# Expert slots of one fixed size, replaced by slots of falling sizes that the experts fill in the order of their token counts

## The chip, the cores and the metric

The kernel runs on one core of one Trainium2 chip. The metric is the device time of a run in microseconds: 519.92 us for the kernel before, the median of 3 runs (519.81 to 520.16). The profiled execution has a span of 518.1 us from its first instruction to its last.

## What is computed

A linear recurrence over 768 steps (4 batches, 8 heads, 48 values a head) makes 3072 rows of 384 values. A two-level gate then sends each row to one of 16 experts, and each expert is two matrix products with a ReLU between them. Cut to what matters:

```python
# recurrence, for each of 768 steps t
y[:, :, t] = r_t @ (state + (u * k_t) outer v_t)
state      = w * state + k_t outer v_t
# bridge: y becomes x, 3072 rows of 384
g_idx = argmax(x @ w_group);  g_w = softmax(x @ w_group)[g_idx]
for g in range(4):
    e_idx = argmax(xg @ w_expert[g]);  e_w = softmax(...)[e_idx]
    for e in range(4):                       # 16 experts in all
        h  = max(xg[mask_e] @ w1[g, e], 0)   # 384 -> 1024
        ye = h @ w2[g, e]                    # 1024 -> 384
        out[tok_idx] = g_w * e_w * ye
```

All numbers are 32-bit floats. How many rows an expert gets depends on the data. With the inputs that the reference sets up, the counts, from the largest to the smallest, are 211, 208, 207, 206, 200, 200, 199, 198, 195, 193, 185, 185, 183, 170, 170 and 162; they add up to 3072.

## The kernel before

The first stage computes the recurrence in 24 tiles of 128 rows, finds the expert of each row, and writes each finished row, by an indirect DMA, to the next free place in the region of its expert in DRAM (`x_sorted`). It keeps running counts in `cum`. A row carries its 384 values, its number and its gate.

```python
CAP = 224
region[e] = RG * e                          # first place of each expert in x_sorted
...
def rows(i):                                # a tile's rows to their places
    nc.gpsimd.indirect_dma_start(out=xs_dram, out_offset=place_i[:, i], in_=xt[:, i, :], ...)
...
for s in range(NT + LAST):                  # NT = 24 tiles; a tile runs through several steps s
    ...
    if s == 18:
        early[0] = load_expert(0, wpool)    # w1 and w2 of expert 0, on the SyncE queue
```

After the loop one number is made: whether an expert has more than 224 rows (or a decay lies outside the supported range). If so, a slow path at the end treats what is left.

```python
pc = ones.T @ cum[:, NT, :]                 # counts on all partitions
left = max(pc - region) >= CAP + 1 ...      # 8 small instructions on VectorE
```

The second stage takes the experts in the order 0 to 15. Each has a slot of 224 columns, in two parts of 128 and 96 rows, whatever its count; places that no token took hold zeros.

```python
NS = [P, CAP - P]                           # 128, 96
def load_rows(e):                           # xg: 3 buffers
    for j, n in enumerate(NS):
        nc.scalar.dma_start(out=xg[0:n, j, :], in_=xs_dram[RG*e + P*j : RG*e + P*j + n, :])
def columns(e):                             # transposes, rows to columns: px on TensorE, xe by VectorE
    ...transpose(px[:, i, P*j : P*j+n], xg[0:n, j, P*ko : P*(ko+1)], ident[0:n, 0:n])
    nc.vector.tensor_copy(xe[:, ...], px)
    # and on VectorE, from xg: ids (row numbers) and gates
def up(e, f):                               # two of 8 blocks of h; 3 matmuls each
    ...matmul(ph[:, i, :], lhsT=w1[:, ko, 128 columns], rhs=xe[:, ko, :])
    nc.scalar.activation(hT[:, f:f+2, :], ph, Relu)
def down(e, d):                             # one of 3 blocks of the output; 8 matmuls
    ...matmul(po, lhsT=w2[:, fo, 128 columns], rhs=hT[:, fo, :])
    nc.scalar.copy(yT[:, d, :], po)
def rows_out(e):                            # transposes back, gate, indirect DMA into out
    ...

load_rows(0); load_rows(1)
weights[1] = load_expert(1, pool)
columns(0)
for e in range(16):
    up(e, 0); up(e, 2)
    if e > 0: rows_out(e - 1)
    up(e, 4); up(e, 6)
    load_rows(e + 2)                        # cut: only where there is such an expert
    down(e, 0); columns(e + 1); down(e, 1); down(e, 2)
    weights[e + 2] = load_expert(e + 2, ...)
rows_out(15)
```

The order of TensorE's instructions is as written here; the other engines' instructions in the second stage are placed by the scheduler. Two sets of weights are held at a time. An expert is 24 matmuls in `up` and 24 in `down`, all with 128-column weights and 224 moving columns; in the trace each of them has two records, so 96 records an expert.

Of the kernel before, what the change touches and what calls it, by code (L numbers as in the profile page):

```python
# [8 lines left out]
FP32 = mybir.dt.float32  # L9
I32 = mybir.dt.int32  # L10
U32 = mybir.dt.uint32
AF = mybir.ActivationFunctionType
# [2 lines left out]

P = 128

CAP = 224

ROW_ID, ROW_GATE, ROW_EXTRA = 0, 1, 2  # L20

# [7 lines left out]
def kernel(  # L29
# [26 lines left out]
    FO = F // P  # L56
    NL = G + GE
    assert N == B * S and DM == H * D and B % 2 == 0 and H % 2 == 0 and S % P == 0 and D <= DP
    assert DM % P == 0 and F % P == 0 and G == Eg == 4 and DM <= 512 and NT * GE <= 512

    NX = N // P + GE
# [193 lines left out]
    def late_constants():  # L255
        nc.vector.tensor_scalar(out=start0, in0=region, scalar1=ident[:, 0:1], scalar2=None, op0=OP.mult)
        nc.vector.tensor_scalar(
            out=desc, in0=iota_f[:, 0:Eg], scalar1=-1.0, scalar2=float(Eg), op0=OP.mult, op1=OP.add
        )
        nc.vector.tensor_copy(cum[:, 0, :], start0)  # L260
        nc.vector.memset(nothing, 0.0)

        wlim = cst([1, H * D], "wlim")
        nc.vector.tensor_scalar(out=wlim, in0=wrow, scalar1=W_LEAST, scalar2=W_MOST, op0=OP.max, op1=OP.min)
        nc.vector.tensor_tensor(out=wlim, in0=wlim, in1=wrow, op=OP.is_equal)
        two = cst([1, 2], "two")
        nc.vector.reduce_sum(out=two[:, 0:1], in_=wlim, axis=AX)
        nc.vector.tensor_scalar(out=two[:, 1:2], in0=two[:, 0:1], scalar1=float(H * D), scalar2=None, op0=OP.is_ge)
        nc.vector.tensor_copy(ok_i, two[:, 1:2])

    def zero_places(j):

# [262 lines left out]
    own(0)  # L535
    todo = {}
    early = {}
    LAST = 5
    for s in range(NT + LAST):
        if s == NT + LAST - 2:  # L540

            for t in [t for t in sorted(todo) if t > s]:
                todo[s].extend(todo.pop(t))
        pieces = todo.pop(s, [])

        def run(when):
            for at, part in pieces:
                if at == when:
                    part()

        if s % 2 == 0 and s // 2 + 2 < NP:
            load_pair(s // 2 + 2)
        if s in (3, 5, 7, 9):
            zero_places(s // 2 - 1)
        if s == 18:
            early[0] = load_expert(0, wpool)
        run("first")
        if s < NT:
            turn(s)
            if s == 0:  # L560
                flipped(1)
                flipped(2)
            if s % 2 == 1 and s // 2 + 1 < NP:
                scale_k(s // 2 + 1, nc.gpsimd)
                own(s // 2 + 1)
        if 0 <= s - 1 < NT:
            own_values(s - 1)
        run("choice")
        if 0 <= s - 4 < NT:
            rows_T(s - 4)  # L570
        n = s - 5
        if 0 <= n < NT:
            row_logits(n)
        if 0 <= s - 3 < NT:
            back(s - 3)
        if 0 <= s - 2 < NT:
            values(s - 2)
        if s % 2 == 0 and s // 2 < NP:
            own_sum(s // 2)
        if s == 2:  # L580
            span_decay()
        run("last")
        if 0 <= s - 1 < NT:
            scores(s - 1)
        if s == 0:
            for t in R:
                nc.gpsimd.memset(t, 0.0)
        if s == 2:
            late_constants()
        if n in ROUTED:  # L590
            choice, before, gate, place, rows = routing(n)
            T = ROUTED[n]
            if n >= NT - B:
                choice()
                todo.setdefault(s + 1, []).extend(
                    [("last", part) for part in (before, gate, place)]
                    + [("last", lambda i=i, rows=rows: rows(i)) for i in range(T)]
                )
            else:
                todo.setdefault(s + 1, []).append(("choice", choice))  # L600
                todo.setdefault(s + 2, []).extend([("first", before), ("last", gate), ("last", place)])
                for i in range(T):
                    todo.setdefault(s + 3 + i, []).append(("last", lambda i=i, rows=rows: rows(i)))
    for _, part in todo.pop(NT + LAST):
        part()
    written.close()
    alive.close()


    left_i = cst([1, 1], "left_i", I32)  # L610
    pc = bank([P, GE], "pc")
    nc.tensor.matmul(pc, lhsT=ones, rhs=cum[:, NT, :], start=True, stop=True)
    cnt = cst([1, GE], "cnt")
    nc.vector.tensor_sub(cnt, pc[0:1, :], region[0:1, :])
    left = cst([1, 2], "left")
    nc.vector.reduce_max(out=left[:, 0:1], in_=cnt, axis=AX)
    nc.vector.tensor_copy(left[:, 1:2], ok_i)
    nc.vector.tensor_scalar(
        out=left[:, 1:2], in0=left[:, 1:2], scalar1=-float(2 * N), scalar2=float(2 * N), op0=OP.mult, op1=OP.add
    )  # L620
    nc.vector.tensor_add(left[:, 0:1], left[:, 0:1], left[:, 1:2])
    nc.vector.tensor_scalar(out=left[:, 0:1], in0=left[:, 0:1], scalar1=float(CAP + 1), scalar2=None, op0=OP.is_ge)
    nc.vector.tensor_copy(left_i, left[:, 0:1])


    NS = [P, CAP - P]
    with tc.tile_pool(name="moe", bufs=2, reuse_waits="tile") as pool:
        weights, xgs, xes, keys, hTs, yTs = {}, {}, {}, {}, {}, {}

        def load_rows(e):  # L630
            xg = xgs[e] = pool.tile([P, 2, XW], FP32, tag="xg", bufs=3, name="xg")
            for j, n in enumerate(NS):
                nc.scalar.dma_start(out=xg[0:n, j, :], in_=xs_dram[RG * e + P * j : RG * e + P * j + n, :])

        def columns(e):
            xg = xgs[e]
            xe = xes[e] = pool.tile([P, KO, CAP], FP32, tag="xe", name="xe")
            for ks in (range(0, 2), range(2, KO)):
                px = bank([P, len(ks), CAP], "px")
                for i, ko in enumerate(ks):  # L640
                    for j, n in enumerate(NS):
                        nc.tensor.transpose(  # L642
                            px[:, i, P * j : P * j + n], xg[0:n, j, P * ko : P * (ko + 1)], ident[0:n, 0:n]
                        )
                nc.vector.tensor_copy(xe[:, ks[0] : ks[-1] + 1, :], px)  # L645
            ids = pool.tile([P, 2], U32, tag="ids", bufs=4, name="ids")
            gates = pool.tile([P, 2], FP32, tag="gates", bufs=4, name="gates")
            for j, n in enumerate(NS):
                nc.vector.tensor_scalar(
                    out=ids[0:n, j : j + 1], in0=xg[0:n, j, DM + ROW_ID : DM + ROW_ID + 1], scalar1=float(N),  # L650
                    scalar2=None, op0=OP.add,
# [4 lines left out]
        def up(e, f):  # L656
# [1 line left out]
            if f == 0:  # L658
                hTs[e] = pool.tile([P, FO, CAP], FP32, tag="hT", name="hT")
            w1, xe = weights[e][0], xes[e]  # L660
            ph = bank([P, 2, CAP], "ph")
            for i in range(2):
                for ko in range(KO):
                    nc.tensor.matmul(  # L664
                        ph[:, i, :], lhsT=w1[:, ko, P * (f + i) : P * (f + i + 1)], rhs=xe[:, ko, :],
                        start=(ko == 0), stop=(ko == KO - 1), skip_group_check=True,
                    )
            nc.scalar.activation(hTs[e][:, f : f + 2, :], ph, AF.Relu)  # L668

        def down(e, d):  # L670

            if d == 0:
                yTs[e] = pool.tile([P, KO, CAP], FP32, tag="yT", name="yT")
            w2, hT = weights[e][1], hTs[e]
            po = bank([P, CAP], "po")
            for fo in range(FO):
                nc.tensor.matmul(  # L677
                    po, lhsT=w2[:, fo, P * d : P * (d + 1)], rhs=hT[:, fo, :], start=(fo == 0), stop=(fo == FO - 1)
                )
            nc.scalar.copy(yTs[e][:, d, :], po)  # L680

        def rows_out(e):
            yT, (ids, gates) = yTs.pop(e), keys.pop(e)
            for j, n in enumerate(NS):
                pb = bank([P, DM], "pb")
                for d in range(KO):
                    nc.tensor.transpose(pb[0:n, P * d : P * (d + 1)], yT[:, d, P * j : P * j + n], ident)  # L687
# [11 lines left out]
            tc.add_to_no_dep_group("rows out", ins.ins)  # L699

        with tc.manual_schedule(engines={mybir.EngineType.PE}):
            for e in range(2):
                load_rows(e)
            weights[0] = early.pop(0)
            weights[1] = load_expert(1, pool)
            columns(0)
            for e in range(GE):
                up(e, 0)
# [3 lines left out]
                up(e, 4)  # L712
                up(e, 6)
                if e + 2 < GE:
                    load_rows(e + 2)
                down(e, 0)
                if e + 1 < GE:
                    columns(e + 1)
                down(e, 1)
                down(e, 2)  # L720
                if e + 2 < GE:
                    weights[e + 2] = load_expert(e + 2, pool if e % 2 else wpool)
            rows_out(GE - 1)

    more = nc.values_load(left_i[0:1, 0:1], min_val=0, max_val=1, skip_runtime_bounds_check_because="a comparison")
    with tc.If(more > 0, preferred_fallthrough_block=False):  # L726
        with tc.tile_pool(name="rest", bufs=1) as rest:
            room = rest.tile([P, 1], FP32, name="room")
            nc.vector.memset(room, float(CAP))
            ok = nc.values_load(  # L730
                ok_i[0:1, 0:1], min_val=0, max_val=1, skip_runtime_bounds_check_because="a comparison"
            )
# [80 lines left out]
            ends = tl([P, GE], "ends")  # L813
            nc.vector.tensor_copy(ends, pc)
            begins = tl([P, GE], "begins")
            nc.vector.tensor_scalar(out=begins, in0=region, scalar1=room[:, 0:1], scalar2=None, op0=OP.add)
            nx = tl([P, GE], "nx")
            nc.vector.tensor_sub(nx, ends, begins)
            nc.vector.tensor_scalar(out=nx, in0=nx, scalar1=0.0, scalar2=float(P - 1), op0=OP.max, op1=OP.add)
# [117 lines left out]
```

## Time and profile before

| what | value |
|---|---|
| time, median of 3 runs | 519.92 us |
| span of the profiled execution | 518.1 us |
| TensorE busy, matmuls | 472.7 us, 91% |
| VectorE, ScalarE, GpSimdE busy | 32%, 27%, 24% |
| moved by DMA | 85.88 MB, 166 GB/s over the span |
| mean granted TensorE clock | 0.961 of full speed |
| first stage: last scatter to `x_sorted` starts at | 186.79 us |
| second stage: first transpose, first `up` matmul start at | 192.44, 195.12 us |
| last indirect DMA to the output starts at | 510.81 us |

A row of the costliest groups reads: line, engine, operation, tiles written and read, shape and number of instructions, then busy time in us and the mean of one in ns, then the engine's idle time just before them and what ended it. The busy times of overlapping records of a group are not counted twice, so a group's busy time may be far below number times mean: matmuls follow each other before the earlier one has drained. The timeline merges neighbouring records of a kind; its first two columns are the start and the duration in us.

### The profile page before, as it was taken

What the parts mean: (1) busy time and instruction counts of PE and PEld (TensorE: products, weight loads), DVE (VectorE), ACT (ScalarE), POOL (GpSimd) and SP (SyncE); (2) the same over time, 40 slices, a digit from 0 to 9 for tenths busy, and PEclk for the clock granted to TensorE, in tenths of its full rate; (3) what the DMA queues carried; (4) which work ended last, traced back from release to release, by engine and by line L of the source; (5) the groups of instructions that cost most, each with busy time, mean ns of one, the idle gap of its engine ahead of it and who ended that gap; (6) DMA issues with size and microseconds to landing.
All of it is one profiled execution on the core that took longest, in us unless ns stands there. A gap on an engine that the chain in (4) does not pass through costs nothing. (4 is left out here: it accounts for less than half of the span.)

```text
span 518.1 us, 8753 instructions
## 1 busy us (share of the span) xinstructions
PE 472.7 (91%) x3533; PEld 454.6 (88%) x3533; DVE 165.1 (32%) x493; ACT 138.1 (27%) x400; POOL 124.7 (24%) x113
## 2 busy tenths in 40 slices
PE   1679999999999629999999999999999999999992
PEld 1568988899999518999999999999999999999992
DVE  4377577877685721011011011011011011010000
ACT  1446545555554201111111111111111111111110
POOL 1874445555543230011011011011011011011011
PEclk9889999999999657999999999999999999999997
DMA  9978989557005441564674574574574564464000
GB/s 193 221 165 206 200 194 198 142 120 279 32 34 184 152 158 42 190 244 153 191 245 156 191 246 152 191 244 150 190 246 150 190 245 151 163 225 147 1 27 26
DMA packets 110613, 85.88 MB, mean 166 GB/s; under 512 B 78475, under 2 KB 102161, under 8 KB 110566
## 3 DMA queue, kind: packets, MB, share of 16 engines
q1 hardware_dynamic: 93228, 63.71, 41.9%
q10 hardware_dynamic: 14010, 12.09, 8.8%
q0 software_dynamic: 3328, 9.47, 5.1%
q8 instruction: 29, 0.48, 0.4%
q14 instruction: 18, 0.15, 0.1%
HBM read 70.25 MB, written 15.78 MB: 166 GB/s over the span
## 5 line engine op out<-in xcount | busy, mean ns | idle before, releaser
L664 PE MATMUL ph<-xe,w 128*128 128x224 f32 x768 | 153.2, 357 | 1.1 <-DVE xe L645 1.1
L677 PE MATMUL po<-hT,w 128*128 128x224 f32 x768 | 150.7, 353 | 0.0
L664 PEld LDWEIGHTS ph<-xe,w 128*128 128x128 f32 x768 | 146.3, 193 | 1.9 <-DVE xe L645 1.4
L677 PEld LDWEIGHTS po<-hT,w 128*128 128x128 f32 x768 | 144.2, 190 | 0.0
L694 POOL DMA_INDIRECT out_dram<-yt,ids x32 | 30.6, 956 | 293.4 <-DVE yt L689 288.5
L668 ACT ACTIVATE hT<-ph 128x448 f32<-128x448 f32 x64 | 34.8, 544 | 138.3 <-PE ph L664 138.3
L689 DVE TENSOR_SCALAR yt<-pb,gates 128x384 f32<-128x384 f32 (+1 forms) x32 | 18.2, 611 | 167.0 <-PE pb L687 167.0
L680 ACT COPY yT<-po 128x224 f32<-128x224 f32 x48 | 16.6, 346 | 134.7 <-PE po L677 99.0
L416 ACT ACTIVATE dv<-vt,du 128x48 f32<-128x48 f32 x192 | 45.9, 324 | 2.2 <-DVE du L410 2.2
L645 DVE COPY xe<-px 128x448 f32<-128x448 f32 (+1 forms) x32 | 14.7, 502 | 66.5 <-PE px L642 66.5
L405 POOL TENSOR_TENSOR dg<-rt,kt 128x768 f32<-128x768 f32 x12 | 22.0, 1831 | 49.3 <-DVE du L410 49.0
L446 DVE TENSOR_TENSOR am<-pa,later 128x512 f32<-128x512 f32 x48 | 30.9, 685 | 7.0 <-PE pa L441 6.7
L441 PE MATMUL pa<-rT,kT 48*128 48x128 f32 x384 | 29.3, 288 | 2.3 <-DVE rT L429 1.5
L360 POOL DMA_INDIRECT x_sorted<-xt,place_i x24 | 23.8, 992 | 28.1 <-DVE rb L316 13.6
L463 PE MATMUL py<-am,vt 128*64 128x128 f32 x384 | 28.3, 285 | 1.8 <-DVE am L446 1.7
L441 PEld LDWEIGHTS pa<-rT,kT 48*128 48x128 f32 x384 | 24.4, 190 | 4.5 <-DVE rT L429 1.7
L463 PEld LDWEIGHTS py<-am,vt 128*64 128x64 f32 x384 | 21.9, 140 | 5.6 <-DVE am L446 2.5
L431 ACT COPY kT<-pk 128x512 f32<-128x512 f32 x24 | 14.1, 588 | 46.2 <-PE pk L427 37.6
L400 POOL TENSOR_TENSOR kh<-kt,T 128x768 f32<-128x768 f32 (+1 forms) x12 | 21.7, 1806 | 12.9 <-ACT T L204 10.9
L406 POOL TENSOR_TENSOR dg<-dg,ub 128x768 f32<-128x768 f32 x12 | 21.8, 1819 | 0.9
L457 PE MATMUL py<-rT,R 128*128 128x128 f32 x160 | 21.3, 276 | 0.4 <-DVE at L354 0.4
L389 PEld LDWEIGHTS rb<-gw,xT 128*128 128x128 f32 x144 | 19.2, 203 | 2.9 <-issue 2.9
(112 smaller groups left out, 389.2 us busy)
## 6 DMA issues: line engine op xcount, KB each, us to landing
w<-in_moe_w_dram SPq DMA_DIRECT2D x32, 1536.0 KB, 6.4
x_sorted<-nothing ACTq DMA_DIRECT2D x4, 1351.0 KB
rt<-in_r_dram SPq DMA_DIRECT2D x12, 384.0 KB, 6.4
vt<-in_v_dram SPq DMA_DIRECT2D x12, 384.0 KB, 7.7
kt<-in_k_dram SPq DMA_DIRECT2D x10, 384.0 KB, 5.7
xg<-x_sorted ACTq DMA_DIRECT2D x16, 193.0 KB, 2.6
xg<-x_sorted ACTq DMA_DIRECT2D x16, 144.8 KB, 3.4
kt<-in_k_dram ACTq DMA_DIRECT2D x2, 384.0 KB, 5.5
```

What stands on the lines that cost most here:

```text
L360: ins = nc.gpsimd.indirect_dma_start(out=xs_dram, out_offset=bass.IndirectOffsetOnAxis(ap=place_i[:, i : i + 1], axis=0), in_=xt[:, i, :], ...
L400: engine.tensor_mul(khs[g % (RING - 1)][:, a0:a1, :, 0:D], kts[g % RING][:, a0:a1], spread(T2[m], 1, a1 - a0))
L405: nc.gpsimd.tensor_mul(dg, rts[g % RING][:, :, :, 0:D], kts[g % RING])
L406: nc.gpsimd.tensor_mul(dg, dg, spread(ub, 1, 2))
L416: nc.scalar.mul(dv[:, h, :], vts[g % (RING + 1)][:, a, h, 0:D], dvs[g][:, a, h : h + 1])
L441: nc.tensor.matmul(pa[e][:, hc, :], lhsT=kT[rows, hc, :], rhs=rT[rows, hc, :], start=True, stop=True, skip_group_check=True,)
L446: nc.vector.tensor_mul(am[:, e], pa[e], spread(later, 1, HP))
L463: nc.tensor.matmul(py[DP * e : DP * (e + 1), hc, :], lhsT=vt[:, a, 2 * hc + e, :], rhs=am[:, e, hc, :], start=(c == 0), stop=True, skip_gr ...
L664: nc.tensor.matmul(ph[:, i, :], lhsT=w1[:, ko, P * (f + i) : P * (f + i + 1)], rhs=xe[:, ko, :], start=(ko == 0), stop=(ko == KO - 1), ski ...
L668: nc.scalar.activation(hTs[e][:, f : f + 2, :], ph, AF.Relu)
L677: nc.tensor.matmul(po, lhsT=w2[:, fo, P * d : P * (d + 1)], rhs=hT[:, fo, :], start=(fo == 0), stop=(fo == FO - 1))
L694: ins = nc.gpsimd.indirect_dma_start(out=out, out_offset=bass.IndirectOffsetOnAxis(ap=ids, axis=0), in_=yt, in_offset=None, bounds_check=N ...
```

## The change

The sixteen slots get fixed, falling sizes. On the chip, the experts are sorted by their counts, and the largest expert takes the largest slot, and so on. Which expert a slot holds is then known only at run time, so the addresses of its rows in `x_sorted` and of its weights come from registers that are loaded from the sorted list. The slots are sized so that fewer columns are computed, while the largest of them has more room than before. The weights of the first slot have to start loading before all counts are known, so its expert is picked from the counts of the first 16 tiles and kept first.

```diff
-CAP = 224
+SLOTS = [256, 240, 229, 220, 214, 212, 206, 202, 199, 196, 193, 190, 187, 184, 178, 173]
+CAP = max(SLOTS)
+FOUR = 4
...
+    def key_constants():                        # once, in step 2
+        nc.vector.scalar_tensor_tensor(out=key_base, in0=region, scalar=-float(GE), in1=iota_f[:, 0:GE], ...)
+        nc.vector.tensor_scalar(out=key_base, in0=key_base, scalar1=float(GE - 1), ...)
+        for i, n in enumerate(SLOTS):
+            nc.gpsimd.memset(most[:, i : i + 1], ...)
+    def token_keys(i):                          # count * 16 + (15 - expert), on all partitions
+        nc.tensor.matmul(pc[:, 0, :], lhsT=ones, rhs=cum[:, i, :], start=True, stop=True)
+        nc.vector.scalar_tensor_tensor(out=pc[:, 1, :], in0=pc[:, 0, :], scalar=float(GE), in1=key_base, ...)
+    def pick_first():
+        keys = token_keys(FOUR * B)
+        nc.vector.reduce_max(out=top, in_=keys, axis=AX)
+        nc.vector.tensor_scalar(out=is_first, in0=keys, scalar1=top, scalar2=FIRST, ...)
+        nc.vector.tensor_copy(first_i, top)
+        number_of(first_i, first_i)             # one more VectorE instruction
...
-        if s == 18:
-            early[0] = load_expert(0, wpool)
+        if s == FOUR * B + 6:                   # 22
+            pieces.append(("last", pick_first))
+        if s == FOUR * B + 7:                   # 23
+            early[0] = load_expert(expert_of(first_i[0:1, 0:1], (SP,)), wpool)
...
+    keys = token_keys(NT)                       # after the last tile
+    nc.vector.tensor_add(keys, keys, is_first)
+    nc.vector.max(out=sorted_key[:, 0:8], in_=keys)
+    nc.vector.match_replace(out=keys, in_to_replace=sorted_key[:, 0:8], in_values=keys, imm_value=-1.0)
+    nc.vector.max(out=sorted_key[:, 8:16], in_=keys)
+    nc.vector.tensor_copy(order_i, sorted_key)
+    number_of(order_i, order_i)
+    ... # then the comparison with the room of each slot, in place of that with CAP
-    NS = [P, CAP - P]
+        def parts(e):
+            return [P, SLOTS[e] - P]
-        def load_rows(e):
+        def load_rows(e, engine, queue):
+            expert = expert_of(number(e), (engine,))        # register load
...
-                nc.scalar.dma_start(out=xg[0:n, j, :], in_=xs_dram[RG * e + P * j : RG * e + P * j + n, :])
+                queue.dma_start(out=xg[0:n, j, :], in_=by_expert[bass.ds(expert, 1), P * j : P * j + n, :]...)
... # transposes, up, down and rows_out: CAP -> SLOTS[e], NS -> parts(e)
-            for e in range(2):
-                load_rows(e)
+            load_rows(0, ACT, nc.scalar)
+            load_rows(1, ACT, nc.scalar)
-            weights[1] = load_expert(1, pool)
+            weights[1] = load_expert(expert_of(number(1), (SP,)), pool)
...
-                    load_rows(e + 2)
+                    expert = load_rows(e + 2, SP, nc.sync)
...
-                    weights[e + 2] = load_expert(e + 2, pool if e % 2 else wpool)
+                    weights[e + 2] = load_expert(expert, pool if e % 2 else wpool)
```

The slow path at the end is changed to know the room of each slot.

## The prediction

> **What bounds the kernel now.** I read the page's busy line first, then busy time by stretch, then the timeline of one expert.
>
> ```profile
> PE 472.7 (91%) x3533; PEld 454.6 (88%) x3533; DVE 165.1 (32%) x493; ACT 138.1 (27%) x400; POOL 124.7 (24%) x113
> L664 PE MATMUL ph<-xe,w 128*128 128x224 f32 x768 | 153.2, 357 | 1.1 <-DVE xe L645 1.1
> L677 PE MATMUL po<-hT,w 128*128 128x224 f32 x768 | 150.7, 353 | 0.0
> ```
>
> The two groups are the experts' products: 153.2 + 150.7 = 303.9 us of a 518.1 us span, with 1.1 us of idle time ahead of them. The busy time by stretch (stretch, its length, busy us of PE, PEld, DVE, ACT and POOL, granted clock, DMA share, GB/s) shows the same:
>
> ```profile
> 190.00:208.00 18.00, 14.47 (x59) 13.38 (x60) 2.44 (x18) 2.18 (x4) 0.00 (x0) 0.70 0.27 78
> 230.00:250.00 20.00, 20.00 (x114) 19.90 (x113) 2.94 (x9) 3.33 (x8) 1.92 (x2) 1.00 0.59 201
> 450.00:500.00 50.00, 50.00 (x279) 49.76 (x278) 5.25 (x10) 8.95 (x19) 5.74 (x6) 1.00 0.34 114
> ```
>
> From about 207 us to the end TensorE is never idle, at full clock, while the DMA engines are at 0.59 and the others below a fifth. So in this stage the time is TensorE's, and the question is what sets the pace of its matmuls: the moving columns, which the change cuts, or the weight loads, which it keeps. A busy PEld alone does not tell, since loads wait for the matmuls ahead of them. The timeline does:
>
> ```profile
> 493.38 0.82 PE L687 MATMUL pb<-ident,yT 128*128 128x128 f32 x6
> 498.57 9.24 PE L677 MATMUL po<-hT,w 128*128 128x224 f32 x48
> ```
>
> Of 48 records in 9.24 us the last ends 0.353 us after it starts (mean of the group), so starts are (9.24 - 0.353) / 47 = 0.189 us apart with 224 columns. With 128 columns it is (0.82 - 0.274) / 5 = 0.109 us. The slope is (0.189 - 0.109) / 96 = 0.83 ns a column. Half of the 128-column records also load 128 columns of weights, so a weight load fits in 0.109 us: down to 128 columns it is not the limit. The smallest slot has 173.
>
> **What the Trainium skill says.** "TensorE: Matmul & The Clock Gate", section "Back-to-back issue gap", gives N/2.4 + 2.5 ns warm for one pass. A record here takes 189 ns for 224 columns, which is 2 x 224/2.4 + 2.5 = 189.2: the trace agrees if a 32-bit record is two passes. The same section also gives sustained figures of about 81 ns at 128 columns and 131 at 512, a slope of only 0.13 ns a column; the 109 and 189 ns of this trace do not follow it, and the trace decides. The section "LDWEIGHTS (loading the stationary operand)" gives columns/1.2, an estimate of 107 ns for 128 columns, just what the 109 ns above allow. "DMA: Bandwidth & Descriptors", section "Why a DMA increments its semaphore by 16 and not by 1", says that a transfer is split over the largest number of engines, up to 16, that divides its slowest dimension. With parts of 128 and 96 rows nothing in the trace before could show this; it matters for a rival below.
>
> **The change, part by part.**
>
> *Removed: columns.* The slots add up to 3279 columns, before they were 16 x 224 = 3584: 305 fewer. Each costs 0.83 ns in each of an expert's 96 records: 305 x 96 x 0.83 ns = 24.3 us, all on TensorE, so all on the path. An expert now takes 96 x 0.189 + about 1.3 us of transposes = 19.4 us, which is the distance of equal points in the timeline. The last slot, with 173 columns, should take 96 x (0.189 - 51 x 0.00083) + 1.3 = 15.4 us, the first, with 256, 22.0 us. The transposes stay: back-transposes move 128 columns whatever the slot, and those into columns are six short ones an expert.
>
> *The slots hold.* All counts of these inputs lie at or below their slots, with the expert that leads after 16 tiles put first (206 rows in 256; then 211 in 240, 208 in 229, 207 in 220 and so on, 162 in 173; the tightest have 3 to 5 places free). So the slow path at the end stays off, as before.
>
> *Added in the first stage.* Two VectorE instructions and 16 tiny GpSimdE memsets in step 2, and five VectorE instructions of about 0.17 us with one matmul in step 22. GpSimdE idles up to 6.7 us a few steps later, and at step 22 TensorE has other tiles' work. I take 0.3 us for all.
>
> *Added between the stages.* The sort is seven VectorE instructions up to the order, some 0.2 us each going by their neighbours (0.15 to 0.18 us): from the last place at 186.0 us to about 187.5. A register load takes about 0.5 us here (0.47 to 0.54 us at the end of the program). The rows cannot be read before the last scatter has landed anyway, at 189.8. So the sort itself is hidden. What it moves is not:
>
> ```profile
> 189.81 5.10 ACTq L633 DMA_DIRECT2D xg<-x_sorted  x8
> 192.44 1.59 PE L642 MATMUL px<-ident,xg 128*128 128x128 f32 x6 [7.99 <-DMA xg<-x_sorted]
> 194.32 0.15 DVE L649 TENSOR_SCALAR ids<-xg 128x1 uint32<-128x1 f32 x1 [1.26 <-DMA xg<-x_sorted]
> 194.45 0.91 DVE L645 COPY xe<-px 128x448 f32<-128x448 f32 x2
> 195.12 12.10 PE L664 MATMUL ph<-xe,w 128*128 128x224 f32 x48 [1.09 <-DVE xe L645]
> ```
>
> TensorE starts the experts only after VectorE's copy at 194.45, and that copy stood behind an instruction that waited for the rows of the *second* expert, landed at 194.3. The instruction order of the changed kernel has the same order on VectorE. Before, the second expert's weights were under way by 156 and 169 us, and the row loads had the DMA engines to themselves. Now these 3.1 MB can start only once the order is known, around 189 us, and run beside the row loads. In the middle of the stage, where rows do run beside weights, they take a median of 3.4 and up to 4.7 us to land, against 2.6 for the first at 189.8. With the register load ahead of the second expert's rows (0.5 us), I put the start of the experts 2 us later, at about 197. The cold clock of this stretch (0.70) costs the same as before.
>
> *Moved: the first slot's weights*, from step 18 (about 120 us) to step 23, where they can start once the pick is made, near 157 us. A half of an expert's weights lands in 6.4 us, so they are there by about 172, over 20 us early.
>
> Sum: 519.9 - 24.3 + 0.3 + 2.0 = 497.9, say 498 us.
>
> **The rivals.**
>
> *The weights become the bound.* An expert's weights are 2 x 1536 KB. SyncE's queue waits for TensorE and not the other way round:
>
> ```profile
> SPq L373 <- PE ph L664: 135.1, 14, 14.4
> SPq L374 <- PE po L677: 129.4, 14, 9.3
> ```
>
> Two halves of 6.4 us[...] need under 13 us, and the shortest slot with a load behind it takes over 16 us. At 0.59 of the DMA engines for 19.4 us the same bytes need about 0.7 at 16.3 us. Against the rival; if it were so, the late slots would stop near 17.5 us and the time would be about 502.
>
> *Row loads on one DMA engine.* Second parts of 101, 71 and 59 rows divide by no number up to 16, so by the skill's rule they would go through one engine. At 201 GB/s and 0.59 busy, an engine moves 201/0.59/16 = 21 GB/s; 101 rows of 1544 bytes are then 7.4 us, 71 are 5.2. They also sit behind half a set of weights (4.7 us) in the same queue, and VectorE has the numbers of slot e+2 ahead of the copy for slot e+1. They would land some 13 us after the start of slot e, which lasts 17 to 18 us there: just hidden. At half that speed each of three slots would stall 1 to 2 us: about 501.
>
> *The weight load sets the pace after all.* Then 173 to 224 columns would gain nothing and 256 would cost: about 521. The 0.109 us records speak against it.
>
> *A longer wait at the start.* If the rows wait behind the whole 3.1 MB (about 9 us), the start moves by up to 5 us: about 501.
>
> **Range and chances.** The 24.3 us are an extrapolation within a measured slope and should hold to half a microsecond; the start could be anywhere from 0.5 to 4 us late, and the rows on one engine may add 3. That gives 495.5 to 501. Faster by over 2% means below 509.5; only a mechanism I have overlooked would miss that: 0.95, within 2% 0.03, slower 0.02.
>
> **What would show it.** Starts of matmuls 0.216 us apart at 256 columns and 0.147 at 173; the two product groups together at about 280 us busy; no idle time ahead of them beyond the first; the first expert matmul near 197 us, with VectorE waiting for the second slot's rows before it; first-stage times unchanged to half a microsecond; row loads of 101, 71 and 59 rows landing later than the others, without a wait on TensorE. Wrong would be gaps in TensorE between slots, a spacing that does not fall below 0.16 us, or a start after 200 us.

## The result, and the profile after

| | before | changed |
|---|---|---|
| time, median of 4 runs each | 519.87 us | 511.61 us |
| ratio of the times, with its 95% interval | | 0.9841 (0.982 to 0.9862) |
| span of the profiled execution | 518.1 us | 509.6 us |
| mean granted TensorE clock | 0.961 | 0.943 |

The change gained 8.3 us, or 1.6%, where 22 us were predicted; to a change within 2% the prediction had given a chance of 0.03. The profile of the changed kernel says first that the expected gain is there. Its busy line and the two groups of the experts' products:

```profile
PE 458.0 (90%) x3535; PEld 433.1 (85%) x3535; DVE 167.3 (33%) x508; ACT 135.5 (27%) x400; POOL 130.1 (26%) x129
...
L736 PE MATMUL ph<-xe,w 128*128 128x256 f32 (+15 forms) x768 | 140.2, 340 | 0.7 <-DVE xe L717 0.7
L749 PE MATMUL po<-hT,w 128*128 128x256 f32 (+15 forms) x768 | 139.0, 338 | 0.0
```

The two groups take 140.2 + 139.0 = 279.2 us, after 303.9: 24.7 us less, for which 24.3 had been predicted. There is no idle time ahead of them but 0.7 us at the first. In the timeline of the changed kernel (start and duration in us), the first and the last slot show the pace:

```profile
224.63 7.08 PE L749 MATMUL po<-hT,w 128*128 128x256 f32 x32
...
492.20 7.20 PE L749 MATMUL po<-hT,w 128*128 128x173 f32 x48
```

With means of 379 and 310 ns for one record, starts are (7.08 - 0.379) / 31 = 0.216 us apart at 256 columns and (7.20 - 0.310) / 47 = 0.147 us at 173, the two numbers of the prediction. From the first expert matmul to the end of the span the kernel takes 301.5 us, before it took 323.0.

But matmuls of `up` begin 13.0 us later: at 208.12 us, after 195.12. That is where most of the gain went. This loss has two parts, found by comparing the starts of equal instructions in both traces. The tiles of the first stage run with a growing delay, 0.8 us at the fourth, 3.6 from the sixth, 6.9 from the twelfth and 7.2 at the last. Then the way from the last matmul of the routing to the first of the experts takes 17.4 us (190.69 to 208.12), after 11.7 (183.44 to 195.12): 5.7 more.

*The first stage.* Busy time by stretch (columns: stretch, length, busy us of PE, PEld, DVE, ACT, POOL, granted clock, DMA share, GB/s), for the kernel before:

```profile
38.00:45.00 7.00, 6.86 (x90) 5.95 (x88) 5.67 (x13) 4.08 (x15) 0.48 (x1) 1.00 0.88 199
...
79.00:86.00 7.00, 6.45 (x83) 5.67 (x80) 5.48 (x16) 3.56 (x13) 3.17 (x2) 1.00 1.21 238
```

and for the changed kernel:

```profile
38.00:45.00 7.00, 5.69 (x33) 5.14 (x35) 4.40 (x10) 3.28 (x14) 0.42 (x1) 0.51 1.03 223
...
79.00:86.00 7.00, 7.00 (x41) 6.78 (x41) 1.59 (x3) 2.75 (x10) 0.00 (x0) 0.51 1.18 181
```

The granted clock is 0.51 in both stretches, and 33 and 41 matmul records stand where there were 90 and 83. By the clock records, two half-clock stretches of 6.8 us (38.1 to 44.9 and 79.0 to 85.8) have been added; one at about 24 us is in both kernels (23.2 to 30.1 before, 24.4 to 31.2 after). What stands around the start of the first added one, in the timeline of the changed kernel:

```profile
37.61 0.84 DVE L285 SCALAR_TENSOR_TENSOR key_base<-region,iota_f 128x16 f32<-128x16 f32 x1
...
38.49 0.17 DVE L288 TENSOR_SCALAR key_base<-key_base 128x16 f32<-128x16 f32 x1
38.57 0.68 DVE L475 TENSOR_TENSOR rT<-pr,T1T 128x512 f32<-128x512 f32 x1
...
39.31 2.07 PE L487 MATMUL pa<-rT,kT 48*128 48x128 f32 x14 [2.52 <-DVE rT L475]
```

TensorE waits 2.52 us for `rT`, in the kernel before 1.54 us at the same place:

```profile
37.71 1.16 PE L441 MATMUL pa<-rT,kT 48*128 48x128 f32 x14 [1.54 <-DVE rT L429]
```

The two constants of the sort stand ahead of `rT` in VectorE's order and take the 1.0 us by which the wait is longer. But the clock fell at 38.06 us, within that wait. Without the two constants `rT` would have been there 1.0 us sooner, which lets TensorE start at about 38.3 us (an estimate from these lines), so up to 38.06 us it would have waited all the same. The 3.41 us before the fall, with TensorE busy for 1.98 us:

```profile
34.65:38.06 3.41, 1.98 (x33) 1.71 (x32) 3.25 (x11) 1.27 (x5) 2.28 (x2) 1.00 1.22 178
```

So the added wait lies inside the stretch and did not begin it. The 16 memsets on GpSimdE ran earlier, at 29.3 us; what they add was not tried apart.

*Between the stages.* The timeline of the changed kernel, to be held against the five lines of the prediction:

```profile
190.69 0.59 PE L381 MATMUL pre<-cum,ones 128*128 128x16 f32 x2
...
193.82 0.98 POOL L406 DMA_INDIRECT x_sorted<-xt,place_i  x1 [0.30 <-issue]
...
194.37 0.37 SPq L422 DMA_DIRECT2D w<-in_moe_w_dram  x1
...
195.09 0.37 SPq L423 DMA_DIRECT2D w<-in_moe_w_dram  x1
...
199.29 0.87 SPq L701 DMA_DIRECT2D xg<-x_sorted  x2
199.41 2.39 ACTq L701 DMA_DIRECT2D xg<-x_sorted  x4
...
205.03 0.48 PE L714 MATMUL px<-ident,xg 128*128 128x128 f32 x1 [13.33 <-DMA xg<-x_sorted]
...
206.10 0.15 DVE L721 TENSOR_SCALAR ids<-xg 128x1 uint32<-128x1 f32 x1 [0.81 <-DMA xg<-x_sorted]
...
208.12 1.22 PE L736 MATMUL ph<-xe,w 128*128 128x256 f32 x2 [0.67 <-DVE xe L717]
```

and two lines of the kernel before that the prediction does not show:

```profile
183.44 0.59 PE L335 MATMUL pre<-cum,ones 128*128 128x16 f32 x2
...
186.79 0.97 POOL L360 DMA_INDIRECT x_sorted<-xt,place_i  x1 [0.54 <-issue]
```

The second slot's weights (3.1 MB) are issued just after the last scatter. The rows can be read only when that scatter has landed, and the reads begin 5.5 us after its start (193.82 to 199.29); before it was 3.0 us (186.79 to 189.81). The reads themselves then take 5.6 to 6.1 us, before 2.6.

*The transposes.* In the changed kernel the six transposes into columns take twice their time in the last five slots, whose second parts have 62 rows or fewer (0.75 us in every slot of the kernel before but the first):

```profile
392.52 0.68 PE L714 MATMUL px<-ident,xg 128*128 128x128 f32 x6
...
409.50 1.40 PE L714 MATMUL px<-ident,xg 128*128 128x128 f32 x6
```

The first line is that of the slot of 193 columns, with a second part of 65 rows; the second that of 190, with 62. Five slots at 0.65 to 0.7 us are some 3.3 us.

The terms add up: 518.1 - 24.7 (columns) + 7.2 (first stage) + 5.7 (between the stages) + 3.3 (transposes) = 509.6, the span after.

### The profile page after: what moved, and what is told of

Its sections match the earlier page's. It is cut to its first block, busy times and chain, and to the rows that moved or that the text cites. A ratio compares the mean times of both kernels' runs of the same rounds, so it can differ in the third digit from the quotient of the medians.

```text
span 509.6 us, 8928 instructions
## 1 busy us (share of the span) xinstructions
PE 458.0 (90%) x3535; PEld 433.1 (85%) x3535; DVE 167.3 (33%) x508; ACT 135.5 (27%) x400; POOL 130.1 (26%) x129
## 4 chain that ended last, share of the span: by engine, by line
issue 50%; PE 20%; DMA 10%; DVE 10%; POOL 8%; POOLq 0%; ACT 0%; DVEq 0%
DMA out_dram<-yt,ids 9%; POOL out_dram L767 4%; PE py L509 4%; PE pa L487 3%; PE py L503 3%; PE rb L435 2%; PE pb L543 2%; PE pk L473 2%; DVE am L492 2%; PE pr L473 2%; PE pu L520 1%; PE px L430 1%; DVE du L456 1%; POOL kh L446 1%; DMA kt<-in_k_dram 1%
## 5 line engine op out<-in xcount | busy, mean ns | idle before, releaser
L736 PE MATMUL ph<-xe,w 128*128 128x256 f32 (+15 forms) x768 | 140.2, 340 | 0.7 <-DVE xe L717 0.7
L749 PE MATMUL po<-hT,w 128*128 128x256 f32 (+15 forms) x768 | 139.0, 338 | 0.0
L736 PEld LDWEIGHTS ph<-xe,w 128*128 128x128 f32 x768 | 132.2, 192 | 3.6 <-DVE xe L717 1.1
L749 PEld LDWEIGHTS po<-hT,w 128*128 128x128 f32 x768 | 130.7, 190 | 2.2
L762 DVE TENSOR_SCALAR yt<-pb,gates 128x384 f32<-128x384 f32 (+15 forms) x32 | 18.2, 611 | 153.5 <-PE pb L760 153.5
L740 ACT ACTIVATE hT<-ph 128x512 f32<-128x512 f32 (+15 forms) x64 | 32.8, 513 | 132.9 <-PE ph L736 132.9
L753 ACT COPY yT<-po 128x256 f32<-128x256 f32 (+15 forms) x48 | 15.8, 330 | 127.3 <-PE po L749 127.3
L717 DVE COPY xe<-px 128x512 f32<-128x512 f32 (+31 forms) x32 | 13.9, 474 | 58.2 <-PE px L714 58.2
L714 PE MATMUL px<-ident,xg 128*128 128x128 f32 x96 | 15.9, 276 | 13.9 <-DMA xg<-x_sorted 13.9
L477 ACT COPY kT<-pk 128x512 f32<-128x512 f32 x24 | 14.1, 585 | 50.4 <-PE pk L473 41.4
L714 PEld LDWEIGHTS px<-ident,xg 128*128 128x128 f32 x96 | 11.8, 145 | 17.7 <-DMA xg<-x_sorted 14.3
```

What stands on the lines that cost most here:

```text
L714: nc.tensor.transpose(px[:, i, P * j : P * j + n], xg[0:n, j, P * ko : P * (ko + 1)], ident[0:n, 0:n])
L736: nc.tensor.matmul(ph[:, i, :], lhsT=w1[:, ko, P * (f + i) : P * (f + i + 1)], rhs=xe[:, ko, 0 : SLOTS[e]], start=(ko == 0), stop=(ko == K ...
L740: nc.scalar.activation(hTs[e][:, f : f + 2, 0 : SLOTS[e]], ph, AF.Relu)
L749: nc.tensor.matmul(po, lhsT=w2[:, fo, P * d : P * (d + 1)], rhs=hT[:, fo, 0 : SLOTS[e]], start=(fo == 0), stop=(fo == FO - 1),)
```

## The experiments

Several theories could account for the first stage and for the start. A: the new constants move the input buffers by 384 bytes, and the loads are slower there; e1 moves them on to 512 bytes, e2 moves those of the kernel before by 128. K: the two constants on VectorE lengthen a wait of TensorE, and the clock falls. W: the second slot's weights slow the last scatter and the rows. S: TensorE pays for going back and forth between transposes of 128 and of few rows. A rival of W is that only the reads of rows suffer from the weights, and the scatter before them does not.

The diffs are against the kernel named in each heading. e7, e8 and e9 hold an unused constant, as e1 does, that sets the place of the input buffers.

**Changed kernel, input buffers moved on (e1), and the kernel before, the same (e2).**

```diff
+    pad = cst([P, 32], "pad")        # 128 bytes a partition that nothing uses
```

> The changed kernel with one unused constant of 128 bytes a partition, nothing else. In the changed kernel new constants moved the input buffers of the first stage by 384 bytes[...]. Theory A (the place of the buffers slows the loads, and the loads the first stage): the first stage gets back most of its 7 us, about 505.5 us. Rival B (14% more zeros are written to DRAM, 1544 instead of 1351 KB four times) and rival C (the added instructions on GpSimdE and VectorE): no change, 511.6 us.

> The kernel before with the same unused constant of 128 bytes, which moves its input buffers[...]; nothing else changes. Theory A: 5 to 7 us slower, about 526 us, with r and v loads landing later from the first microseconds on. Rivals B and C: no change, 519.9 us.

e1: 514.28 us, ratio 0.9846 (0.9783 to 0.9909), that of the changed kernel, where A had put 505.5 us. e2: 521.63 us, ratio 1.0001 (0.9977 to 1.0025). The loads did follow the place of the buffers. In the second fortieth of the span the DMA engines moved 221 GB/s before and 155 with the change; e1 brought it back to 223, and e2 lowered that of the kernel before to 155. The time followed in neither, and both half-clock stretches stayed in e1. A fell: these loads are off the path.

**Changed kernel, rows of the third slot issued ahead of the second slot's weights (e3).**

```diff
             weights[0] = early.pop(0)
+            third = load_rows(2, SP, nc.sync)
             weights[1] = load_expert(expert_of(number(1), (SP,)), pool)
```

> The changed kernel with the rows of the third slot ahead of the weights of the second slot in SyncE's program, so that these 3.1 MB wait until the last scatter has landed. Theory W (the weights, started at 194.4 us, hold up the last scatters, which landed 2.7 us later than before, and then the first rows): the first expert matmul starts 4 to 6 us earlier and the time is about 506.5 us. Rival (the rows are late because of the register loads and the register addresses): the start moves by under 1 us, about 511.5 us.

509.95 us, ratio 0.9775 (0.9712 to 0.9837), which is between the two expectations. As the row load waits for the scatters, so do the weights behind it. The last scatter then landed in 2.8 us, as before the change. But the weights, issued at 197.50 us, now met the second half of the rows, which landed only at 202.25, and the first expert matmul came 15.2 us after the last routing matmul (17.4 with the change). So the slowed scatter is one part of the wait, against the rival of W, and the rows are the other.

**Changed kernel, transposes grouped by part (e4).**

```diff
-                for i, ko in enumerate(ks):
-                    for j, n in enumerate(parts(e)):
+                for j, n in enumerate(parts(e)):
+                    for i, ko in enumerate(ks):
```

> The changed kernel with the six transposes of a slot in another order: both parts no longer alternate within a PSUM bank, all 128-row ones of a bank come first and then the short ones. In the last five slots (62 rows or fewer in the second part) the six transposes take 1.4 us instead of 0.7. Theory S (what costs is each change between a 128-row transpose and one of at most 64 rows): changes per slot fall from 5 to 3, some 0.25 us for each of five slots, about 510.3 us. Rival (each short transpose is slow by itself): 511.6 us, the six still at 1.4 us.

509.92 us, ratio 0.9766 (0.9706 to 0.9827). The whole time cannot decide over 1.5 us: the changed kernel itself has a ratio of 0.9841 on one chip and 0.9772 (0.9739 to 0.9805) on another (e5). The lines do. In e4, for the slot of 190 columns:

```profile
407.36 1.11 PE L714 MATMUL px<-ident,xg 128*128 128x128 f32 x6
```

1.08 to 1.11 us in all five slots, after 1.35 to 1.40. The same six transposes in an order with fewer changes of size cost 0.3 us less: S holds. Single records of this slot show where the time goes. In e4 the two places where the size stays the same have starts 0.11 us apart, be it 128 rows or 62; at the three changes of size it is 0.20, 0.16 and 0.26 us. In the changed kernel all five steps are changes, at 0.20 to 0.26 us. Short transposes are thus not slow by themselves. Against the 0.68 us of the slot before, it is 0.72 us for five changes and 0.43 for three, 0.14 us for one.

**Changed kernel, again (e5); key constants in step 14 in place of step 2 (e6); kernel before with the key constants in step 2 (e7).** These and the next kernel ran on one chip.

```diff
+        if s == 14:
+            key_constants()
         ...
         if s == 2:
             late_constants()
-            key_constants()
```

> The changed kernel once more, unaltered, so that the others of this call stand beside it on one chip. 511.6 us was measured for it; 511 to 514 us here.

> The changed kernel with the key constants (two VectorE instructions, 16 GpSimdE memsets) made in step 14 instead of step 2. Theory K: in step 2 they lengthen TensorE's wait at 37 us from 1.5 to 2.5 us, that window then counts as idle, and the next 6.8 us run at half clock, a loss of about 3.5 us; without them the half clock from 38 to 45 us vanishes and the time falls by about 3 us against the unaltered one. Rival: TensorE is idle enough around 37 us in any case and the half clock comes or not by the phase of the clock's windows: under 1 us.

> The kernel before with that one part of the change alone: the key constants in step 2 (their results unused)[...]. Theory K: about 3 us slower than the kernel before, with a half clock from about 38 us. Rival: same as before within 1 us.

e5: 510.64 us, the median of five runs (a sixth, in a slow state of the chip with a mean clock of 0.74, took 616.14 us and is left out). e6: 507.26 us, ratio 0.9733 (0.9698 to 0.9768), 3.4 less than e5, though this interval overlaps that of e5. e7: 523.41 against 521.37 us, ratio 1.0041 (1.0021 to 1.0061): the constants alone make the kernel before 2 us slower. In e6's busy time by stretch:

```profile
38.00:45.00 7.00, 6.88 (x77) 6.44 (x77) 4.46 (x11) 4.51 (x17) 0.22 (x1) 0.76 1.02 228
...
79.00:86.00 7.00, 6.58 (x84) 6.05 (x83) 4.58 (x15) 4.56 (x19) 1.79 (x1) 1.00 1.17 154
```

and TensorE's wait for `rT` is 1.37 us. In the timeline of e7 the first instruction of `key_base` takes 1.38 us, and TensorE's wait is 2.05 us:

```profile
37.60 1.38 DVE L277 SCALAR_TENSOR_TENSOR key_base<-region,iota_f 128x16 f32<-128x16 f32 x1
...
39.84 1.44 PE L457 MATMUL pa<-rT,kT 48*128 48x128 f32 x10 [2.05 <-DVE rT L445]
```

K holds in part. That the constants in step 2 cost time is shown: 2 us in e7, and e6 points the same way. They do it by a wait that is 0.5 us (e7) to 1.0 us (changed kernel) longer and, as far as the traces show it, by a longer stretch of half clock. This lasts 3.4 us in the two traces that have them in step 14, and 6.8 or 10.2 us in all that have them in step 2. But K has them begin it, and that does not hold. In e7 the stretch runs from 35.4 us, before the first instruction of `key_base` at 37.60. For its start the rival named with e6, the phase of the clock's windows, stays open; its bound of under 1 us for the time fell. The mean clocks of all runs bound its share. By them e7 spends on average 43.8 us at half clock and the kernel before 41.4, e5 53.7 and e6 49.2. Half-clock time loses at most half of itself, so this is at most 1.2 us of the 2 us of e7 and 2.2 us of the 3.4 us of e6.

How far the first stage is late goes with these clock stretches in every trace but that of e10 (delay of the first instruction of the last tile against the profiled run of the kernel before). Each trace, that of the kernel before too, also has a stretch of 3.4 to 10.2 us that begins between 22.9 and 25.7 us.

| trace | half-clock stretches that begin between 34 and 100 us | last tile later by |
|---|---|---|
| before; e11 | none; none | 0; 0.9 us |
| e9; e6 (key constants later) | 40.0-43.4; 38.4-41.8 | 1.8; 1.9 us |
| e2; e8; e3; e4 | 38.8-45.7; 36.0-46.2; 35.8-46.0; 35.8-46.1 | 4.3; 4.7; 5.0; 5.0 us |
| changed; e1; e7; e5 | 38.1-44.9; 38.3-45.1; 35.4-45.7; 39.2-46.0, and each a second one of 6.8 us from 79.0 to 80.2 | 7.2; 7.6; 7.6; 8.3 us |

Three things limit it. The first stretch can come without the key constants too: e2's profiled run had it (524.98 us, clock 0.955), where the median of its runs is 521.63 us. The profiled run of e7, 526.28 us, is one of the three slowest of its 15, so its 7.6 us are not what the constants cost. And the second stretch, near 79 us, came in four traces, and not in three others of the changed kernel that had the first one and the same first-stage instructions (e3, e4, e8); TensorE's wait ahead of it is 0.74 us in the changed kernel, with no new instruction near. Why it came is open.

**Changed kernel, second slot's weights held back until that slot's rows have landed (e8).** The register with the expert's number is loaded from a value that VectorE makes of the order and, times zero, of a number in the rows.

```diff
-            weights[1] = load_expert(expert_of(number(1), (SP,)), pool)
             columns(0)
+            nc.vector.tensor_copy(second_f, order_i[0:1, 1:2])
+            nc.vector.scalar_tensor_tensor(out=second_f, in0=xgs[1][0:1, 0, DM + ROW_ID : ...],
+                scalar=0.0, in1=second_f, op0=OP.mult, op1=OP.add)
+            nc.vector.tensor_copy(second_i, second_f)
+            weights[1] = load_expert(expert_of(second_i[0:1, 0:1], (SP,)), pool)
```

> The changed kernel in which the number of the second slot's expert, as SyncE reads it for that slot's weights, is made to depend on a value of the second slot's rows: the 3.1 MB start only once these rows have landed. Theory W in its strict form (every microsecond of the late start beyond the first stage's own is the weights' traffic ahead of the scatters and rows): from the last routing matmul to the first expert matmul 12 us as in the kernel before (11.7), not 17.4; about 5 us faster than the unaltered one. Rival: register loads and register addresses cost it: under 2 us faster.

503.43 us, ratio 0.967 (0.9629 to 0.971), 7.2 less than e5. The timeline of e8 at the start of the experts:

```profile
191.27 0.98 POOL L408 DMA_INDIRECT x_sorted<-xt,place_i  x1 [0.30 <-issue]
...
194.39 2.32 ACTq L703 DMA_DIRECT2D xg<-x_sorted  x4
...
196.93 1.84 PE L716 MATMUL px<-ident,xg 128*128 128x128 f32 x6 [7.76 <-DMA xg<-x_sorted]
...
199.69 9.55 PE L738 MATMUL ph<-xe,w 128*128 128x256 f32 x35 [0.92 <-DVE xe L719]
...
200.64 0.37 SPq L424 DMA_DIRECT2D w<-in_moe_w_dram  x1
```

Rows are read 3.1 us after the last scatter's start and are there 2.5 us later. From the last routing matmul (188.15) to the first expert matmul it is 11.5 us, the 11.7 of the kernel before. The weights start only at 200.64 us, and still TensorE has no wait for them: they land by 212.1 us, and the second slot starts at about 223. W holds, and with the register loads still there its rival is out. The start is 6.6 us shorter than in e5's trace (18.1 us, from 191.73 to 209.80, against 11.5). e8's trace also lacks the second clock stretch, so this is not to be set against the 7.2 us to half a microsecond.

**Changed kernel with all three amendments (e9).** The edits of e4, e6 and e8 together.

> The changed kernel with the three amendments together: key constants made in step 14, the second slot's weights held back until its rows have landed, and transposes grouped by part so that those of 128 rows and those of few rows do not alternate. If the three losses are separate (clock windows in the first stage, scatter and rows slowed by the weights, alternating transposes), their gains add: from 503.4 us with the weights held back, about 3.7 less for the constants and 1.5 less for the transposes, so about 498 us, ratio 0.955 to 0.96. In its trace: no half-clock stretch near 38 us longer than one window of 3.4 us, first-stage tiles within 2 us of the kernel before, 11 to 12 us from the last routing matmul to the first expert matmul, and transposes into columns at about 1.1 us in the last five slots. If they overlap (a gain in the first stage is taken back at the wait between the stages), it stays at 501 or above.

497.08 us, ratio 0.9531 (0.9493 to 0.957). The losses were separate: the last tile is 1.8 us late, the start takes 10.9 us, and the transposes of the five small slots 1.08 to 1.11 us.

```profile
193.97 1.83 PE L717 MATMUL px<-ident,xg 128*128 128x128 f32 x6 [7.67 <-DMA xg<-x_sorted]
...
196.15 12.72 PE L739 MATMUL ph<-xe,w 128*128 128x256 f32 x48 [0.36 <-DVE xe L720]
```

**Kernel before with slots of 212 columns (e10), and with its zeros written in parts of 56 rows (e11).** This isolates the columns: no sort, no registers. 212 is still above the largest count, 211.

```diff
-CAP = 224
+CAP = 212
         ...
-        part = CAP // 4                # e11 only
+        part = 56
         nc.scalar.dma_start(out=regions[part * j : part * (j + 1)], in_=spread(nothing[0:part, :], 1, GE))
```

> The kernel before with 212 columns in each of its 16 slots, in place of 224, and nothing else: no sort, no registers, no pick. 16 x 12 = 192 columns fewer, which by the measured slope is 192 x 96 x 0.83 ns = 15.3 us, so about 505 us on a chip where the kernel before takes 520 to 521, ratio 0.970 to 0.972; the two product groups each about 7.5 us shorter, the first stage and the wait between the stages as in the kernel before. That would be below the changed kernel's 511 with less change. If columns are worth less when nothing else is changed, or if second parts of 84 rows cost something by themselves (transposes, row loads on fewer engines), it stays above 508.

> The 212-column kernel again, with the zeros written in four parts of 56 rows a region, as in the kernel before, in place of 53. If the 689 us of the run before came from these four writes alone (53 has no divisor up to 16 but 1, each write took some 51 us at 25 GB/s and held ScalarE's next instructions back), they land in a few us as before, the first stage is back at the times of the kernel before, and the time is 519.9 - 15.3, about 505 us by the columns (up to 1.6 less by what the two product groups of that run measured, 287.5 us in place of 303.9), ratio 0.968 to 0.972. If something else in the smaller slots held the first stage up, it stays far above 510.

e10: 689.17 us, ratio 1.3209 (1.3169 to 1.3248). That is above 508, but for none of the reasons that the expectation gives. The two product groups fell as expected (144.3 and 143.2 us), and the first stage lost 186 us. ScalarE's part of the timeline of e10:

```profile
97.69 52.47 ACTq L275 DMA_DIRECT2D x_sorted<-nothing  x1
...
150.25 0.59 ACT L431 COPY kT<-pk 128x512 f32<-128x512 f32 x1 [52.00 <-issue]
```

Issuing the second, third and fourth of the four writes of zeros takes 44 to 52 us each (0.3 to 0.4 in the kernel before), and ScalarE's next copy stands behind it. A part is now 212 / 4 = 53 rows, before it was 56. The Trainium skill, "DMA: Bandwidth & Descriptors", section "Why a DMA increments its semaphore by 16 and not by 1", says that a transfer is shared by the largest number of engines, up to 16, that divides its slowest dimension: 14 for 56 and 1 for 53. The trace agrees so far as it shows: if a write moves its 1278.6 KB in the 51 us or so that the next is held up, that is some 25 GB/s, where all DMA engines together moved 221 early in the kernel before.

e11: 505.04 us, ratio 0.969 (0.9653 to 0.9727), in the expected range, and the zeros were all of it. From its first expert matmul (195.6 us) to the end at 503.1 it takes 307.5 us, the kernel before 323.0: 15.5 us for 192 columns, predicted 15.3. The pace in e11:

```profile
484.08 8.76 PE L677 MATMUL po<-hT,w 128*128 128x212 f32 x48
```

(8.76 - 0.343) / 47 = 0.179 us. So with these counts twelve columns less in every slot gave more than the changed kernel as it stands, with none of its losses; with the losses mended (e9) the sorted slots are 8 us better than that.

## Why the prediction was wrong

**The term of the columns was right.** Of 24.3 us predicted 24.7 came, at the pace and by the slope that the prediction took from 128 and 224 columns; e11 confirms it by itself. The rivals of weights as a bound and of the weight load as the pace are out: no idle time ahead of the groups, and 0.147 us at 173 columns.

**The term "I take 0.3 us for all" for the first stage failed: the stage was 7.2 us later.** The step summed the durations of the added instructions, and looked for slack on GpSimdE and on TensorE, but not at VectorE's order in step 2, where a late `rT` was already holding TensorE. There the two constants delay TensorE by their full 1.0 us in the changed kernel, and the run by 2 us (e7) to some 3.4 us (e6). The step also took the clock of this stage as given, and two stretches of 6.8 us at half clock were added, around each of which the tiles fell back by some 3 us. The Trainium skill, "TensorE: Matmul & The Clock Gate", section "What's actually happening", says that the gate looks at free-running windows of about 3.4 us. The trace agrees in the length: 6.8 us are two such windows, 3.4 in e6 and e9 one. Its table wants an idle window of that length; here TensorE was busy for 1.98 of the 3.41 us ahead of the first stretch and waited for 1.3 us at most in one piece, and the trace decides. What begins the first stretch stays open, since it comes without the constants in e2 and ahead of them in e7, and the second has no shown cause. So by e7 and e6 the constants account for 2 to 3.4 of the 7.2 us, and the rest is not explained.

**The term "I put the start of the experts 2 us later" was too small: 5.7 us.** Its mechanism was right, weights beside rows, and its size was taken from rows that run beside weights later in the stage (3.4 to 4.7 us; here 5.6 to 6.1). It held the landing of the last scatter, which nothing had been beside before, for fixed; the weights slowed that too, by 2.5 us. e8, which parts them, restores the start. With the late first stage it came to 208.12 us, past the 200 us that the prediction had named as a sign of being wrong. The rival of a longer wait, up to 5 us by rows behind the weights, was nearest, and left the scatter out as well.

**"The transposes stay" failed by 3.3 us.** Six short instructions a slot were taken as fixed. At 62 rows and fewer beside 128 they doubled; e4 shows that the changes of size cost it, at 0.14 us each.

**The sort and the rows on one DMA engine were right.** The order was ready at 193.7 us, before the scatter had landed. Loads of 101, 71 and 59 rows made VectorE wait 5.8, 3.3 and 3.7 us for their numbers (other loads from the third slot on up to 3.5 us), and TensorE not at all.

The range failed with the sum: it allowed 0.5 to 4 us for the start and 3 for the rows, and nothing for the first stage or the transposes. Its own terms together reach 519.9 - 24.3 + 0.3 + 4 + 3 = 502.9 us, past the 501 that it states. What lay outside the bounding stage had been priced by the durations of instructions alone.

## What to carry to other kernels

When a change adds small instructions to an engine that feeds TensorE, look up in the timeline what follows them there and whether TensorE is already waiting for it. A load that a change releases at a new moment must be held against all transfers in flight then, also those whose landing starts the next step; letting it start later can be the faster order. When a size changes, check every count derived from it: parts of transposes, and the rows of a transfer.

## What the runs showed of the hardware

- Half-clock stretches that begin between 22 and 100 us last 3.4, 6.8 or 10.2 us in all traces but that of e10. One followed 3.41 us in which TensorE was busy for 1.98 us, though the same code at times escapes it.
- An indirect write that landed in 2.7 us took 5.3 beside 3.1 MB of weights.
- Six transposes of 128 rows alternating with 62 or fewer took 1.35 to 1.40 us, with 65 rows 0.68, and grouped 1.08 to 1.11. Starts are 0.16 to 0.26 us apart where the size changes, and 0.11 where it stays. Why 65 rows escape it is open.
- Beside writes of 53 rows times 16 regions, the issue of the next such write held ScalarE up to 52 us; with 56 rows 0.4 us.
- Moving the input buffers by 128 or 384 bytes changed the early loads from 221 to 155 GB/s, by 512 bytes to 223, and the time by nothing measurable.
